# Windowed attention into a three-way maxout layer on one core: x of chunk 1 scaled between masks, V of chunk 2 loaded behind weight 2, half a y moved ahead of products with V

## The chip, the cores and the metric

The kernel runs on one core of one Trainium2 chip. The metric is the time of one execution on the device in microseconds (us). The engines are named as in the profile: PE (matrix products), PEld (its weight loads, which overlap PE), DVE (vector), ACT (scalar, activation), POOL (GpSimd) and SP (which issues most of the transfers).

## The reference

Attention of 4 batches, 8 heads, 768 tokens and head size 64, in which a query sees the first 4 keys (the sink) and the last 128 keys up to itself; its output, 3072 tokens of 512 values, goes through a layer that takes the maximum of three products and then a last product.

```python
scores = scale * np.matmul(q, k.transpose(0, 1, 3, 2))
keep = is_sink | in_window                       # first 4 keys, or 0 <= i - j < 128
a = softmax(np.where(keep, scores, -1000000000.0))
x = np.matmul(a, v).transpose(0, 2, 1, 3).reshape(B * S, H * D)
h = np.maximum(np.maximum(x @ w1, x @ w2), x @ w3)   # 512 -> 768
out = h @ w_out                                       # 768 -> 512
```

## The kernel before

The tokens are worked in 12 chunks of 256, three to a batch. For a chunk, the steps are these, each with a helper that emits its instructions.

- `load` issues the transfers of q, k and V of a chunk on SP, 512 KB each, into raw tiles of which there are two per kind. A `gate` is a tiny write by POOL into the tile; SP's transfer has to wait for it. The gate `after(wi, c)` copies one value of weight `wi` (counted from 0) at column `c`, so it opens only when that piece of the weight has landed.
- `load_w` and `load_wo` load the three weights in thirds, and the output weight in halves, on POOL's queue, which also turns them into bf16.
- `cast_qk` and `cast_v` turn raw tiles to bf16 on POOL, ACT or DVE; `turn` transposes q or k on PE and copies the result out of PSUM; later chunks are transposed by a transfer (`turn_dma`).
- `score` multiplies keys with queries for a pair of heads (p from 0 to 3); `expo` takes two exponentials per pair on ACT; `mask` multiplies by a 0/1 mask on DVE. Pairs 0 and 1 of chunk 1, and the pairs of chunk 0, are masked ahead of their scores by a product with the identity (`premask`), and need no `mask`. `sink_score` and `sink_v` do the same for the four sink keys.
- `av_open` takes four PSUM banks, the o tiles, and writes the sink's share; `av` adds the products of a pair with V, whose last column is one and so gives the row sums. Then DVE takes the reciprocal (L476) and scales x (L479), and the bank is returned.
- `xpose` transposes x in four blocks of 128 columns, one per pair, for each of two halves of the chunk, and copies them to xT (L493).
- `ffn_h(ci, fp, wi)` makes 8 products of 256 columns of chunk `ci`, a third `fp` of the 768 columns and weight `wi` (L517). For weight 0, ACT copies them to h (L523); for the others DVE takes the maximum with h (L527).
- `ffn_y(ci, t)` makes half a chunk of output, 6 products of 512 columns (L540), copied to y by ACT or DVE (L542).

All engines run the written order of the program: the calls stand in one list by hand, each engine takes its own instructions from it in that order, and waits at the first whose operands aren't there. The change edits this list from chunk 1's products with V (L706) to chunk 3's scores (L810). From chunk 4 on a loop repeats one order per chunk.

PSUM has eight banks, shared by everything that PE writes. `bank` takes the one that was returned first, `give` returns it in the order of the program, and the taker waits on the chip until the last reader of the former content is done:

```python
def bank(shape, dtype, name):
    j = free.pop(0)
```

So a call that is moved shifts which bank each later call gets, and on whose reading it depends.

Of the kernel before, what the change touches and what calls it, by code (L numbers as in the profile page):

```python
# [16 lines left out]
def kernel(  # L17
# [13 lines left out]
    nc = tc.nc  # L31
# [12 lines left out]
    DS = d_model // 128  # L44
# [4 lines left out]
    with tc.manual_schedule():  # L49
# [43 lines left out]
        def load(ci, what="kqv", gate=None, part=None, parts=1, eng=None):  # L93
            if ci >= NCH:
                return
            b, c = divmod(ci, CPB)
            t0 = c * 256
            for w in what:
                src = {"k": k, "q": q, "v": v}[w]
                if (ci, w) not in raws:  # L100
                    raws[ci, w] = raw.tile([128, H, 2, D], F32, tag=w + "_raw", name=w + "_raw")
                dst = raws[ci, w]
                if gate is not None:
                    gate(dst[0:1, 0, 0, 0:1])
                n = H // parts
                for g in range(parts) if part is None else (part,):
                    (eng or nc.sync).dma_start(
                        out=dst[:, n * g:n * g + n],
                        in_=src[b, n * g:n * g + n, t0:t0 + 256]
                            .rearrange("h (p i) d -> p h (i d)", i=2))  # L110
# [102 lines left out]
        addm0 = const.tile([128, 3, 128], BF16, name="addm0")  # L213
# [75 lines left out]
        def load_w(wi, c0=0, c1=None):  # L289
            c1 = d_ff if c1 is None else c1  # L290
            w = (moe_w1, moe_w2, moe_w3)[wi]
            nc.gpsimd.dma_start(out=w_sb[wi][:, :, c0:c1],  # L292
                                in_=w.rearrange("(a p) f -> p a f", p=128)[:, :, c0:c1])
# [107 lines left out]
        def mask(ci, p, eng=None):  # L401
            if ci >= NEW:
                return mask4(ci, p)
            lo = 0 if ci % CPB else 1
            e = es[ci, p][0]
            (eng or nc.vector).tensor_mul(e[:, :, lo:], e[:, :, lo:], msk0[0] if lo else msk)  # L406
# [36 lines left out]
        os_ = {}  # L443

        def av_open(ci):
            b, c = divmod(ci, CPB)
            for p in range(NP):
                os_[ci, p] = bank([128, 2, 2, D + 1], F32, "o")
            if c:
                for t in range(2):  # L450
                    for p in range(NP):
                        hp = slice(32 * p, 32 * p + 32)
                        nc.tensor.matmul(  # L453
                            os_[ci, p][:, t], lhsT=es[ci, "sink"][hp, t], rhs=vs[b % 2][hp],
                            start=(t == 0), stop=False, skip_group_check=True,
                            tile_position=(32 * p, 0))

        xs = {}

        def av(ci, p):  # L460
            b, c = divmod(ci, CPB)
            o = os_[ci, p]
            e = es[ci, p][0]
            first = c == 0
            for t in range(2):
                for a in range(2):
                    blocks = [(1, ci, 0)] if t == 0 else [(2, ci, 0), (3, ci, 1)]
                    if t == 0 and c:
                        blocks = [(0, ci - 1, 1)] + blocks
                    for s, cv, n in blocks:  # L470
                        nc.tensor.matmul(  # L471
                            o[:, t, a], lhsT=e[:, a, s], rhs=vb[cv % RING][:, n, 2 * p + a],
                            start=first, stop=True, skip_group_check=True)
                        first = False
            rc = work.tile([128, 2, 2], F32, tag="rc", bufs=4, name="rc")
            nc.vector.reciprocal(rc, o[:, :, :, D])  # L476
            if ci not in xs:
                xs[ci] = work.tile([128, NP, 2, 2, D], BF16, tag="x", bufs=2, name="x_sb")
            nc.vector.tensor_mul(xs[ci][:, p], o[:, :, :, 0:D],  # L479
                                 rc.unsqueeze(3).to_broadcast([128, 2, 2, D]))  # L480
            give(o)

        xTs = {}

        def xpose(ci, t, eng=None):
            eng = eng or nc.scalar
            if t == 0:
                xTs[ci] = work.tile([128, DS, 2, 128], BF16, tag="xT", bufs=3, name="xT")
            pt = bank([128, DS, 128], BF16, "xt")
            for ds in range(DS):  # L490
                nc.tensor.transpose(
                    pt[:, ds], xs[ci][:, ds, t].rearrange("q a d -> q (a d)"), ident)
            (nc.scalar.copy if eng is nc.scalar else eng.tensor_copy)(xTs[ci][:, :, t], pt)  # L493
            give(pt)
# [6 lines left out]

        hs = {}

        def ffn_h(ci, fp, wi, cuts=1, eng=nc.scalar):
            if ci not in hs:
                hs[ci] = work.tile([128, FB, 256], BF16, tag="h", bufs=3, name="h_sb")
            hp = bank([128, 2, 256], F32, "h_ps")
            for f in range(2):
                c0 = (2 * fp + f) * 128
                for ds in range(DS):  # L510
                    x = xTs[ci][:, ds]
                    if ci < NEW:
                        x = x.rearrange("q t (i r) -> q i t r", i=2)
                    else:
                        x = (x.rearrange("q t c -> q (t c)")
                             .rearrange("q (j i r) -> q i j r", i=2, r=32))
                    nc.tensor.matmul(  # L517
                        hp[:, f].rearrange("q (i t r) -> q i t r", i=2, r=x.shape[3]),
                        lhsT=w_sb[wi][:, ds, c0:c0 + 128], rhs=x,
                        start=(ds == 0), stop=(ds == DS - 1))  # L520
            dst = hs[ci][:, 2 * fp:2 * fp + 2]
            if wi == 0:
                (nc.scalar.copy if eng is nc.scalar else eng.tensor_copy)(dst, hp)  # L523
            else:
                for f in range(cuts):
                    x = slice(2 * f // cuts, 2 * (f + 1) // cuts)
                    nc.vector.tensor_max(dst[:, x], dst[:, x], hp[:, x])  # L527
            give(hp)
# [177 lines left out]
        expo(1, 2)  # L706
        load_w(2, 256, 512)
        load_w(2, 512, 768)
        mask(1, 3)
        ffn_h(0, 1, 0)  # L710
        mask(1, 2)
        av_open(1)
        ffn_h(0, 0, 0)
        av(1, 0)
        load(2, 'v', gate=after(0, 300))
        av(1, 3)
        av(1, 1)
        av(1, 2)
        ffn_h(0, 2, 1)
        ffn_h(0, 1, 1)  # L720
        xpose(1, 0, nc.vector)
        xpose(1, 1, nc.scalar)
        ffn_h(0, 0, 1)
        cast_qk(2, 'k', 1, nc.gpsimd)
        ffn_h(1, 2, 0)
        cast_qk(2, 'k', 0, nc.scalar)
        ffn_h(1, 0, 0)
        ffn_h(1, 1, 0)
        load_wo()
        load(3, 'q', gate=after(2, 300))  # L730
        load(3, 'k')
        factors(msk0[0], addm0)
        turn(2, 'k', 0, nc.vector)
        ffn_h(1, 0, 1)
        cast_v(2, 1, 0, nc.gpsimd)
        turn(2, 'k', 1, nc.scalar)
        ffn_h(1, 1, 1)
        cast_qk(2, 'q', 1, nc.scalar)
        cast_qk(2, 'q', 0, nc.vector)
        ffn_h(1, 2, 1)  # L740
        ffn_h(1, 1, 2)
        turn(2, 'q', 1, nc.scalar)
        ffn_h(0, 0, 2)
        turn(2, 'q', 0, nc.scalar)
        ffn_h(0, 1, 2)
        score(2, (0,))
        expo(2, 0)
        score(2, (3,))
        score(2, (1,))
        cast_v(2, 1, 1, nc.gpsimd)  # L750
        sink_score(2)
        expo(2, 1)
        mask(2, 0)
        load(3, 'v', gate=after(1))
        cast_v(2, 0, 0, nc.gpsimd)
        expo(2, 3)
        ffn_h(1, 0, 2)
        cast_v(2, 0, 1, nc.gpsimd)
        ffn_h(0, 2, 2)
        ffn_h(1, 2, 2)  # L760
        score(2, (2,))
        load(4, 'q', gate=after(0, 300))
        cast_qk(3, 'q', 0, nc.gpsimd)
        av_open(2)
        load(4, 'k', gate=after(0))
        mask(2, 1)
        expo(2, 2)
        cast_qk(3, 'k', 0, nc.gpsimd)
        load(4, 'v')
        mask(2, 3)  # L770
        mask(2, 2)
        cast_qk(3, 'q', 1, nc.vector)
        ffn_y(0, 0)
        ffn_y(0, 1)
        av(2, 0)
        turn(3, 'q', 0, nc.scalar)
        cast_qk(3, 'k', 1, nc.scalar)
# [3 lines left out]
        av(2, 3)  # L781
        turn(3, 'q', 1, nc.scalar)
        av(2, 1)
        ffn_y(1, 0)
        turn(3, 'k', 1, nc.scalar)
        turn(3, 'k', 0, nc.scalar)
        xpose(2, 0, nc.scalar)
        xpose(2, 1, nc.vector)
        ffn_y(1, 1)
        cast_qk(4, 'q', 1, nc.vector)  # L790
        cast_v(3, 0, 0, nc.gpsimd)
        cast_v(3, 0, 1, nc.gpsimd)
# [5 lines left out]
        cast_qk(4, 'k', 0, nc.vector)  # L798
        cast_qk(4, 'k', 1, nc.gpsimd)
        mask(3, 1)  # L800
        ffn_h(2, 0, 0)
        cast_v(4, 1, 0, nc.gpsimd)
        cast_v(3, 1, 0, nc.vector)
        score(3, (3,))
        turn_dma(4, 'k')
        turn_dma(4, 'q')
        expo(3, 0)
# [173 lines left out]
```

## Time and profile before

| | us |
|---|---|
| median of 3 runs | 176.03 |
| lowest and highest | 175.41 and 176.61 |
| the profiled execution | 175.3 |
| its span, first to last instruction | 173.6 |
| PE busy | 167.1 |
| DVE busy | 124.7 |
| POOL busy | 110.9 |
| ACT busy | 88.7 |
| bytes moved | 35.22 MB, 203 GB/s over the span |

The profile is of one execution. Line numbers are those of the kernel before. A group row has the line, engine, operation, tiles written and read, shapes and count, then its busy time, the mean of one in ns, and the idle time ahead of it with what ended it. A row of the timeline has start, duration (of so many instructions together), and in square brackets the idle time ahead. The times of one engine can overlap a little, since a row covers an instruction from its first to its last cycle. A row of a transfer ends with the us from issue to landing.

### The profile page before, as it was taken

To read this page: it belongs to the slowest core of one execution; us is meant where nothing else is said; L and a number is where in the kernel's file an instruction comes from. 1 tells how busy PE (TensorE), PEld (TensorE's weight loads), DVE (VectorE), ACT (ScalarE), POOL (GpSimd) and SP (SyncE) were. 2 spreads that over 40 slices of the span, in tenths; PEclk is the share of its full clock that TensorE was granted. 3 is DMA by queue.
4 is the path that set the end of the run, shared out by engine and by line. 5 is a ranking of instruction groups with operands and counts; after the bars stand their busy time and mean duration, and the time that the engine had idled before them with its cause. 6 is when DMAs were issued, how large, how long until landed. Compare 5 with 4: busy or idle time off the path is not lost.

```text
span 173.6 us, 5416 instructions
## 1 busy us (share of the span) xinstructions
PE 167.1 (96%) x2225; PEld 128.6 (74%) x2225; DVE 124.7 (72%) x262; ACT 88.7 (51%) x183; POOL 110.9 (64%) x193
## 2 busy tenths in 40 slices
PE   7979999999999999999999999999999999999992
PEld 2546888857696697797797797797797896896871
DVE  3387854796797985986877976877777776776361
ACT  4778544677954614817726717717636516510210
POOL 7399507545499999999999999999998600000000
PEclk9999999999999999999999999999999999999999
DMA  4999999999999997988999999989999119017303
GB/s 139 301 288 198 218 217 256 221 306 276 280 195 216 190 273 124 245 199 216 253 199 252 195 224 246 265 168 227 264 195 259 32 33 377 21 34 272 121 2 121
DMA packets 71545, 35.22 MB, mean 203 GB/s; under 512 B 27488, under 2 KB 69984, under 8 KB 71520
## 3 DMA queue, kind: packets, MB, share of 16 engines
q1 hardware_dynamic: 65824, 31.60, 79.0%
q0 software_dynamic: 5552, 3.15, 12.7%
q8 instruction: 17, 0.28, 0.7%
q10 hardware_dynamic: 144, 0.13, 0.2%
q14 instruction: 8, 0.07, 0.1%
HBM read 25.17 MB, written 6.29 MB: 181 GB/s over the span
## 4 chain that ended last, share of the span: by engine, by line
PE 85%; DMA 7%; POOL 5%; issue 1%; DVE 0%; POOLq 0%; SPq 0%
PE h_ps L517 52%; PE y_ps L564 11%; PE y_ps L540 7%; PE o L471 6%; DMA w<-in_moe_w_dram 4%; PE st L357 3%; DMA v_raw<-in_v_dram 3%; PE st L331 2%; POOL w L292 2%; POOL vb L123 1%; PE pt L138 1%; PE o L453 1%; PE y_ps L586 1%; PE sk L423 1%; POOL q_bf L118 0%
## 5 line engine op out<-in xcount | busy, mean ns | idle before, releaser
L517 PE MATMUL h_ps<-xT,w 128*128 128x256 bf16 x864 | 101.2, 273 | 0.2 <-DMA w<-in_moe_w_dram 0.2
L517 PEld LDWEIGHTS <-w 128*128 128x128 bf16 x864 | 81.7, 98 | 10.7 <-issue 0.5
L527 DVE TENSOR_TENSOR h_sb<-h_sb,h_ps 128x512 bf16<-128x512 bf16 (+1 forms) x74 | 49.0, 670 | 17.4 <-PE h_ps L517 15.6
L523 ACT CAST h_sb<-h_ps 128x512 bf16<-128x512 f32 x35 | 20.6, 589 | 51.3 <-PE h_ps L517 51.2
L129 POOL CAST vb<-v_raw 32x512 bf16<-32x512 f32 x48 | 36.8, 766 | 2.5 <-DMA v_raw<-in_v_dram 0.3
L90 POOL CAST k_bf<-k_raw 32x512 bf16<-32x512 f32 x48 | 29.6, 616 | 2.2
L398 ACT ACTIVATE e_sb<-st 128x512 bf16<-128x512 f32 (+1 forms) x48 | 23.1, 583 | 1.1 <-PE st L331 1.1
L479 DVE TENSOR_TENSOR x_sb<-o,rc 128x256 bf16<-128x256 f32 x48 | 20.4, 424 | 1.7
L564 PE MATMUL y_ps<-wo,h_sb 64*64 64x512 bf16 (+1 forms) x312 | 21.1, 377 | 0.0
L471 PE MATMUL o<-vb,e_sb 128*128 128x65 bf16 x352 | 16.5, 193 | 0.8 <-DVE vb L123 0.8
L471 PEld LDWEIGHTS <-e_sb 128*128 128x128 bf16 x352 | 14.5, 97 | 3.1 <-ACT e_sb L398 1.0
L123 POOL CAST vb<-v_raw 64x512 bf16<-64x512 f32 x18 | 12.6, 697 | 5.7 <-DMA v_raw<-in_v_dram 5.1
L389 DVE TENSOR_TENSOR e_sb<-e_part,msk 128x1024 bf16<-128x1024 bf16 x16 | 13.1, 831 | 3.3 <-ACT e_part L374 3.1
L406 DVE TENSOR_TENSOR e_sb<-e_sb,msk 128x1024 bf16<-128x1024 bf16 (+1 forms) x18 | 13.6, 776 | 2.3 <-ACT e_sb L398 2.1
L564 PEld LDWEIGHTS <-h_sb 64*64 64x64 bf16 (+1 forms) x312 | 9.9, 106 | 5.0
L374 ACT ACTIVATE e_part<-st 128x384 bf16<-128x384 f32 x32 | 13.1, 495 | 0.5 <-PE st L357 0.5
L540 PE MATMUL y_ps<-wo,h_sb 128*128 128x512 bf16 x54 | 12.8, 380 | 0.0
L476 DVE RECIPROCAL rc<-o 128x4 f32<-128x4 f32 x48 | 8.4, 174 | 4.0 <-PE o L471 3.8
L118 POOL CAST k_bf<-k_raw 128x512 bf16<-128x512 f32 x6 | 3.8, 650 | 9.5 <-PE pt L138 6.8
L118 ACT CAST q_bf<-q_raw 128x512 bf16<-128x512 f32 x13 | 7.6, 620 | 3.0 <-DMA q_raw<-in_q_dram 3.0
L540 PEld LDWEIGHTS <-h_sb 128*128 128x128 bf16 x54 | 4.8, 98 | 5.4 <-DVE h_sb L527 0.8
L427 ACT ACTIVATE e_sink<-sk 128x256 bf16<-128x256 f32 x8 | 3.1, 389 | 10.0 <-PE sk L423 10.0
(90 smaller groups left out, 142.9 us busy)
## 6 DMA issues: line engine op xcount, KB each, us to landing
k_raw<-in_k_dram SPq DMA_DIRECT2D x11, 512.0 KB, 5.6
v_raw<-in_v_dram SPq DMA_DIRECT2D x11, 512.0 KB, 5.6
q_raw<-in_q_dram SPq DMA_DIRECT2D x10, 512.0 KB, 6.9
out_dram<-y_sb SPq DMA_DIRECT2D x9, 512.0 KB, 3.1
w<-in_moe_w_dram POOLq DMA_DIRECT2D x9, 256.0 KB, 6.1
q_raw<-in_q_dram SPq DMA_DIRECT2D x4, 256.0 KB, 7.6
out_dram<-y_sb SPq DMA_DIRECT2D x1, 1024.0 KB, 5.3
wo<-in_moe_w_out_dram POOLq DMA_DIRECT2D x2, 384.0 KB, 8.0
```

Of the source, the lines that this page charges most:

```text
L90: f(bfs[ci, "k"][x:x + 32, :, n], raws[ci, "k"][y:y + 32, :, i].rearrange("q (p a) d -> q p a d", a=2))
L123: eng.tensor_copy(vb[ci % RING][64 * i:64 * i + 64, n, :, 0:D], raws[ci, "v"][64 * n:64 * n + 64, :, i])
L129: eng.tensor_copy(vb[ci % RING][x:x + 32, n, :, 0:D], raws[ci, "v"][y:y + 32, :, i])
L398: nc.scalar.activation(e[:, a, lo:], st[a][:, lo:], AF.Exp, scale=scale)
L406: (eng or nc.vector).tensor_mul(e[:, :, lo:], e[:, :, lo:], msk0[0] if lo else msk)
L471: nc.tensor.matmul(o[:, t, a], lhsT=e[:, a, s], rhs=vb[cv % RING][:, n, 2 * p + a], start=first, stop=True, skip_group_check=True)
L479: nc.vector.tensor_mul(xs[ci][:, p], o[:, :, :, 0:D], rc.unsqueeze(3).to_broadcast([128, 2, 2, D]))
L517: nc.tensor.matmul(hp[:, f].rearrange("q (i t r) -> q i t r", i=2, r=x.shape[3]), lhsT=w_sb[wi][:, ds, c0:c0 + 128], rhs=x, start=(ds == 0 ...
L523: (nc.scalar.copy if eng is nc.scalar else eng.tensor_copy)(dst, hp)
L527: nc.vector.tensor_max(dst[:, x], dst[:, x], hp[:, x])
L540: nc.tensor.matmul(yp, lhsT=hs[ci][:, fb, t * 128:(t + 1) * 128], rhs=wo[:, fb], start=(fb == 0), stop=(fb == FB - 1))
L564: nc.tensor.matmul(yps[ci][t][c:c + cols], lhsT=hs[ci][hp, fb, x:x + cols], rhs=wo[hp, fb], start=(turn == 0 and fb == 0), stop=(turn == 1 ...
```

## The change

In the list of calls:

- The products with V of chunk 1 move up, those of pairs 0 and 1 ahead of the masks of pairs 3 and 2. The scaling of x is split off as `norm`, and stands between the masks and behind other products. The two transposes of xT take their blocks in the order 0, 1, 3, 2.
- The maximum of `ffn_h(0, 2, 1)` is split off as `ffn_max` and put behind the copies of xT.
- `load(2, 'v')` moves from ahead of the products with V to behind `load_wo` and the mask factors, with a gate on the last third of weight 2 in place of weight 0. The load of V of chunk 3, and those of q and k of chunk 4, move up. Two of the four casts of V of chunk 2 go from POOL to DVE, and the other two move down.
- Groups of h products are reordered: `ffn_h(0, 0, 1)` two groups later, `ffn_h(1, 0, 1)` ahead of the transposes of k, `ffn_h(0, 0, 2)` ahead of a transpose of q, and `ffn_h(1, 0, 2)` ahead of the scores of chunk 2.
- `ffn_y(1, 0)` moves ahead of all products with V of chunk 2, and `ffn_y(1, 1)` ahead of its transposes. `score(3, (3,))` moves ahead of `ffn_h(2, 0, 0)`.

```diff
-        def av(ci, p):
+        def av(ci, p, then=True):
...
+            if then:
+                norm(ci, p)
+
+        def norm(ci, p):
+            o = os_[ci, p]
             rc = work.tile([128, 2, 2], F32, tag="rc", bufs=4, name="rc")
             nc.vector.reciprocal(rc, o[:, :, :, D])
...
-        def xpose(ci, t, eng=None):
+        def xpose(ci, t, eng=None, order=range(DS)):
...
-        def ffn_h(ci, fp, wi, cuts=1, eng=nc.scalar):
+        def ffn_h(ci, fp, wi, cuts=1, eng=nc.scalar, then=True):
...
+            maxima[ci, fp, wi] = hp
+            if then:
+                ffn_max(ci, fp, wi, cuts, eng)
+
+        def ffn_max(ci, fp, wi, cuts=1, eng=nc.scalar):
+            hp = maxima.pop((ci, fp, wi))
             dst = hs[ci][:, 2 * fp:2 * fp + 2]
...
         load_w(2, 512, 768)
+        av_open(1)
+        av(1, 0, then=False)
+        av(1, 1, then=False)
         mask(1, 3)
         ffn_h(0, 1, 0)
+        norm(1, 0)
         mask(1, 2)
-        av_open(1)
+        av(1, 3, then=False)
         ffn_h(0, 0, 0)
-        av(1, 0)
-        load(2, 'v', gate=after(0, 300))
-        av(1, 3)
-        av(1, 1)
-        av(1, 2)
-        ffn_h(0, 2, 1)
+        norm(1, 1)
+        av(1, 2, then=False)
+        norm(1, 3)
+        ffn_h(0, 2, 1, then=False)
+        norm(1, 2)
+        xpose(1, 0, nc.vector, (0, 1, 3, 2))
+        xpose(1, 1, nc.scalar, (0, 1, 3, 2))
+        ffn_max(0, 2, 1)
         ffn_h(0, 1, 1)
-        xpose(1, 0, nc.vector)
-        xpose(1, 1, nc.scalar)
-        ffn_h(0, 0, 1)
         cast_qk(2, 'k', 1, nc.gpsimd)
         ffn_h(1, 2, 0)
         cast_qk(2, 'k', 0, nc.scalar)
         ffn_h(1, 0, 0)
+        ffn_h(0, 0, 1)
         ffn_h(1, 1, 0)
+        ffn_h(1, 0, 1)
         load_wo()
+        factors(msk0[0], addm0)
+        load(2, 'v', gate=after(2, 600))
         load(3, 'q', gate=after(2, 300))
         load(3, 'k')
-        factors(msk0[0], addm0)
+        load(3, 'v', gate=after(1))
         turn(2, 'k', 0, nc.vector)
-        ffn_h(1, 0, 1)
-        cast_v(2, 1, 0, nc.gpsimd)
+        ffn_h(1, 1, 1)
         turn(2, 'k', 1, nc.scalar)
-        ffn_h(1, 1, 1)
...
         ffn_h(1, 1, 2)
+        ffn_h(0, 0, 2)
         turn(2, 'q', 1, nc.scalar)
-        ffn_h(0, 0, 2)
+        ffn_h(0, 1, 2)
         turn(2, 'q', 0, nc.scalar)
-        ffn_h(0, 1, 2)
+        ffn_h(1, 0, 2)
         score(2, (0,))
         expo(2, 0)
         score(2, (3,))
         score(2, (1,))
-        cast_v(2, 1, 1, nc.gpsimd)
         sink_score(2)
         expo(2, 1)
         mask(2, 0)
-        load(3, 'v', gate=after(1))
+        expo(2, 3)
+        load(4, 'q', gate=after(0, 300))
+        load(4, 'k', gate=after(0))
+        cast_v(2, 1, 0, nc.gpsimd)
         cast_v(2, 0, 0, nc.gpsimd)
-        expo(2, 3)
-        ffn_h(1, 0, 2)
-        cast_v(2, 0, 1, nc.gpsimd)
         ffn_h(0, 2, 2)
         ffn_h(1, 2, 2)
         score(2, (2,))
-        load(4, 'q', gate=after(0, 300))
         cast_qk(3, 'q', 0, nc.gpsimd)
         av_open(2)
-        load(4, 'k', gate=after(0))
...
         mask(2, 2)
+        cast_v(2, 1, 1, nc.vector)
+        cast_v(2, 0, 1, nc.vector)
         cast_qk(3, 'q', 1, nc.vector)
         ffn_y(0, 0)
         ffn_y(0, 1)
+        ffn_y(1, 0)
         av(2, 0)
...
         av(2, 1)
-        ffn_y(1, 0)
         turn(3, 'k', 1, nc.scalar)
         turn(3, 'k', 0, nc.scalar)
+        ffn_y(1, 1)
         xpose(2, 0, nc.scalar)
         xpose(2, 1, nc.vector)
-        ffn_y(1, 1)
...
         mask(3, 1)
+        score(3, (3,))
         ffn_h(2, 0, 0)
         cast_v(4, 1, 0, nc.gpsimd)
         cast_v(3, 1, 0, nc.vector)
-        score(3, (3,))
```

More of the change, by code (lines that the diff above doesn't have):

```diff
@@ L489, in xpose @@
             pt = bank([128, DS, 128], BF16, "xt")
-            for ds in range(DS):
+            for ds in order:
                 nc.tensor.transpose(
@@ L502 @@
         hs = {}
-        def ffn_h(ci, fp, wi, cuts=1, eng=nc.scalar):
+        maxima = {}
+        def ffn_h(ci, fp, wi, cuts=1, eng=nc.scalar, then=True):
             if ci not in hs:
```

## The prediction

> **What bounds the kernel now.** I read the page's busy shares and costliest groups first, then a table by stage, then the chain that ended last, and only then single engines around the edited lines.
>
> ```profile
> span 173.6 us, 5416 instructions
> PE 167.1 (96%) x2225; PEld 128.6 (74%) x2225; DVE 124.7 (72%) x262; ACT 88.7 (51%) x183; POOL 110.9 (64%) x193
> L517 PEld LDWEIGHTS <-w 128*128 128x128 bf16 x864 | 81.7, 98 | 10.7 <-issue 0.5
> ...
> 16.80:36.90 20.10, 19.93 (x244) 16.63 (x244) 13.62 (x27) 11.61 (x23) 9.44 (x19) 1.00 1.28 235
> 36.90:46.30 9.40, 9.40 (x105) 5.77 (x105) 6.83 (x18) 7.39 (x15) 4.62 (x8) 1.00 1.06 282
> 46.30:170.20 123.90, 123.90 (x1739) 98.69 (x1737) 94.33 (x186) 58.14 (x124) 84.42 (x135) 1.00 0.85 189
> ```
>
> The stage table's columns are the stretch, its length, and the busy time of PE, PEld, DVE, ACT and POOL, then clock, DMA share and GB/s. All edited lines run between 16.8 and 46.3 us. There PE is idle for 0.17 us in all, and after 46.3 it is never idle. Since a busy PE may still be waiting inside, I check it against the chain (start, length, what):
>
> ```profile
> 16.59 6.10 DMA w<-in_moe_w_dram
> ...
> 22.73 3.67 PE h_ps L517 x32
> ...
> 32.60 0.77 PE st L331 x18
> 33.37 0.22 PE sk L423 x4
> 33.59 2.73 PE h_ps L517 x24
> 36.32 0.33 PE st L331 x6
> 36.65 0.23 PE o L453 x8
> 36.87 2.70 PE y_ps L540 x12
> 39.57 0.24 PE o L471 x8
> ...
> 40.98 1.29 PE y_ps L540 x6
> 42.28 0.45 PE pt L138 x8
> ...
> 44.91 0.98 PE h_ps L517 x8
> ...
> 76.24 4.37 PE h_ps L517 x40
> ```
>
> In the undisturbed stage 40 products of h take 4.37 us, 0.109 us each, so 8 take 0.87. By that measure 32 should take 3.50 and took 3.67, 24 should take 2.62 and took 2.73, 8 took 0.98, and 12 products of y took 2.70 where twice 1.29 is 2.58. The hidden stalls in these rows are about 0.1 us each. **PE's order of work sets the end.** The edit removes no matmul, so it can win only such crumbs, and every new wait of PE before 46.3 goes one for one into the time: behind it there is no gap to absorb it.
>
> **The change, part by part.** I walk PE's new order and ask at each step which operand or PSUM bank comes last. Banks go round first in, first out, in the order of the program, so I replayed takes and returns for the new order by hand.
>
> ```profile
> 16.61 2.11 ACT L398 ACTIVATE e_sb<-st 128x512 bf16<-128x512 f32 x4
> ...
> 17.84 0.69 DVE L406 TENSOR_TENSOR e_sb<-e_sb,msk 128x1024 bf16<-128x1024 bf16 x1 [0.22 <-ACT e_sb L398]
> 19.68 0.18 DVE L476 RECIPROCAL rc<-o 128x4 f32<-128x4 f32 x1 [0.24 <-PE o L471]
> ...
> 20.24 0.17 DVE L476 RECIPROCAL rc<-o 128x4 f32<-128x4 f32 x1
> ...
> 17.15 1.05 PE L517 MATMUL h_ps<-xT,w 128*128 128x256 bf16 x8
> ...
> 21.95 0.61 PE L491 MATMUL xt<-ident,x_sb 128*128 128x128 bf16 x8
> ```
>
> *Chunk 1's products with V ahead, x scaled between the masks.* The opening of the o banks now stands right behind the scores, at 17.15, where an h product stood. Its fourth bank is the one that the first of the four exponentials from 16.61 returns, at about 17.2: **+0.1**. The products of pairs 0 and 1 wait for no mask, since those pairs were masked before their scores. DVE then does mask, scale, mask, scale, scale, scale: from 17.84, with 0.65 for a mask and 0.56 for a scaling (19.68 to 20.24), the last one ends near 17.84 + 2 x 0.65 + 4 x 0.56 = 21.4. PE has from 17.25 the rest of the opening (0.23), four products with V (0.24 each) and three groups of 8 h products (0.87 each), so it reaches the transposes near 21.05, takes blocks 0, 1 and 3 first (0.17), and waits for block 2: **+0.2** (bounds 0, if DVE starts earlier, and 0.5).
>
> *What that wait replaces.* Before, the transposes ended at 21.95 + 0.45 = 22.40, and the next h product started at 22.73, when the last piece of weight 1 landed (16.59 + 6.10). In the new order this piece is first read about 2 us later: **-0.33**. The maximum that is put behind the copy of xT costs nothing by itself: DVE would have to wait for the transposes there, and the bank that it returns is taken only several groups of h products later.
>
> *V of chunk 2 behind weight 2.*
>
> ```profile
> v_raw<-in_v_dram SPq DMA_DIRECT2D x1, 512.0 KB, 11.6
> ...
> DMA to landing us min/median/max: 4.1/5.4/11.6
> ...
> w<-in_moe_w_dram POOLq DMA_DIRECT2D x1, 256.0 KB, 11.4
> ...
> q_raw<-in_q_dram SPq DMA_DIRECT2D x1, 512.0 KB, 8.8
> ...
> 20.54 2.05 SPq L107 DMA_DIRECT2D v_raw<-in_v_dram  x1
> ...
> 29.07 1.08 POOL L238 TENSOR_SCALAR msk<-addm 128x384 bf16<-128x384 bf16 x2
> ...
> 32.30 1.27 POOL L123 CAST vb<-v_raw 64x512 bf16<-64x512 f32 x2 [2.16 <-DMA v_raw<-in_v_dram]
> ...
> 40.44 0.62 POOL L118 CAST k_bf<-k_raw 128x512 bf16<-128x512 f32 x1 [1.13 <-DMA k_raw<-in_k_dram]
> ```
>
> V was issued at 20.54 and landed 11.6 us later, at 32.1. The last piece of weight 2, the last of three issues of about 0.75 us from 17.53, lands at about 19.0 + 11.4 = 30.4, so the new gate opens there, behind the mask factors (1.08 us) on POOL, and V is issued near 30.6. Behind that gate on POOL wait the gates of q and V of chunk 3 and of chunk 4, then the casts; on SP all the later loads. Their places in the ring are the same as before (V2, q3, k3, V3, q4, k4). V is first in an emptied ring, beside the output weight. Landing bounds: 30.6 + 4.1, the shortest that the trace has for V, and 30.6 + 11.6, its longest; by bytes, 0.5 MB at half of the 235 GB/s of this stage is 4.5 us, so I take about 36. Two of the four casts of V move from POOL to DVE, at 0.42 us, the price of the same cast there, behind the masks of chunk 2, and end near 39.8; POOL's two end near 37.3. Half a y, 1.29 us, moved ahead puts the first product with V at about 41.2 instead of 39.57, so the late V lies under y: **0**. Without that cover it would cost what V is later than 39.6.
>
> The Trainium skill, "DMA: Bandwidth & Descriptors", section on queues, rings and completion order, says that each DMA engine takes turns between its queue rows, packet by packet. That speaks against the change: by it V, behind q in SP's row, took nothing from weight 2 while q was there, and holding V back brings no weight sooner; the landings (30.4 for the weight, 32.1 for V) agree. Without it weight 2 could land as soon after its issue as weight 1 did, at 25.1, and the gate would open with the factors' end at 30.1, half a us sooner; the sum is the same by both.
>
> *A group of 8 h products of chunk 1 ahead of the scores of chunk 2.*
>
> ```profile
> 31.00 2.47 DVE L527 TENSOR_TENSOR h_sb<-h_sb,h_ps 128x512 bf16<-128x512 bf16 x4
> ...
> 36.96 2.30 DVE L406 TENSOR_TENSOR e_sb<-e_sb,msk 128x1024 bf16<-128x1024 bf16 x3
> ...
> 33.02 1.09 ACT L398 ACTIVATE e_sb<-st 128x512 bf16<-128x512 f32 x2 [0.67 <-PE st L331]
> ...
> 34.26 2.09 ACT L398 ACTIVATE e_sb<-st 128x512 bf16<-128x512 f32 x4
> ...
> 39.60 0.59 ACT L542 COPY y_sb<-y_ps 128x512 f32<-128x512 f32 x1 [0.70 <-PE y_ps L540]
> 40.09 0.59 ACT L142 COPY qT<-pt 128x512 bf16<-128x512 bf16 x1
> 40.56 0.63 ACT L118 CAST k_bf<-k_raw 128x512 bf16<-128x512 f32 x1
> ```
>
> Let S be the start of those scores, 32.60 before. ACT's sixth exponential of that run ends at 34.26 + 2.09 = 36.35, S + 3.75. Before, PE came to the opening of the o banks at 36.65, S + 4.05, behind 24 h products, and lost nothing. Now only 16 stand there: 0.77 + 0.22 + 1.75 + 0.33 puts PE there at S + 3.07, and its fourth bank is the one that this sixth exponential returns. Three small matmuls go first; then PE waits about 0.6 us, less the 0.11 that the 24 products lost before: **+0.5** (bounds +0.2, if a later maximum on DVE delays the 16 products anyway, and +0.7). This is the largest term.
>
> *The half y ahead.* Before, ACT had cast k of chunk 3 by 40.56 + 0.63 = 41.19, well ahead of its transposes at 42.28. Now the copy of that half y stands in front on ACT: y ends at 37.35 + 3 x 1.29 = 41.2; copy, qT copy and cast, started some 0.48 us apart, end at 41.25 + 0.48 + 0.48 + 0.62 = 42.8; PE, 1.41 us of work after 41.2 (39.57 to 40.98 before), is there at 42.6: **+0.25** (0 to 0.5). The y's own 0.12 of stall goes: **-0.1**. The extra score ahead of the first h of chunk 2 takes up the wait for xT that 0.98 against 0.87 shows: 0. POOL behind its cast of k at 40.44 is 0.3 to 1 us later, gives it back in its next wait for a transfer, and has two casts less.
>
> Sum: 0.1 + 0.2 - 0.33 + 0.5 + 0.25 - 0.1 = **+0.6 us**. The profiled execution took 175.3 us with its span of 173.6; it becomes 175.9. The runs' median is 176.03, 0.7 above the profiled one, so the forecast for a median is 176.6.
>
> **The rivals.** *No new wait holds* (the masks start earlier, the banks come in time): the gains alone, 0.33 and 0.1, give 175.6. For it: the terms rest on walks with margins of 0.1 to 0.3 us. Against it: the exponentials' 3.75 us behind S are a fixed row, and PE has only 3.07 us of work to cover them.
>
> *V comes late* and the forecast turns into a clear loss: if V took 11.6 us again it would land at 42.2, POOL's two casts (1.27 us) end at 43.5, and the first product with V, else at 41.2, waits 2.3 us: 176.6 + 2.3 = 178.9. It decides from a landing after 39.9. For it: q and k behind it took 8.8 us and more. Against it: those stood behind V itself in the ring, and now V is first.
>
> *PE has headroom.* The Trainium skill, "Perfetto Trace Analysis", section on the most contended engine, calls matmul busy time a bad measure and the weight loads' share the better one; here that is 74%. As a mechanism of this kernel: if better order let the edited stage's 17 groups of 8 h products run at the weight load's 98 ns instead of 109, that is 136 x 0.011 = 1.5 us and, with the 0.33, 174.2. Against it: 0.109 holds for 40 in a row where nothing is waited for, so order has nothing to do with it.
>
> *The move of V does nothing that it says*: the weights land as before, and V's delay is hidden; the time is then that of the other terms, 176.6.
>
> **How the numbers follow.** Forecast 0.59, no new wait 0.22, V late 0.11, headroom 0.03, the idle move of V 0.05. One per cent is 1.8 us, about what a measurement of this kernel can tell from no change. Only V late lies above it (0.11), only headroom below it (0.03), the others within (0.86). Terms at their lower ends (0.1, 0, -0.33, 0.2, 0, -0.1) give -0.1, at their upper (0.1, 0.5, -0.33, 0.7, 0.5, 0) +1.5, so the forecast's own range is 175.9 to 177.5. With the rival below, the spread of the runs shown (175.41 to 176.61) and part of the way to a late V, the range is 175.3 to 177.9.
>
> **What would show it.** Right: no wait of PE for a weight near 22.7; a short gap of PE before the third block of xT's first transposes; a gap of about half a us at the opening of the o banks near 37, released by ACT; V landed before 39.9; PE's pieces after 46.3 the same, shifted by about 0.6 us. Wrong: PE waiting for a cast of V near 41, DVE's casts of V later than PE's third half of y, or a stage after 46.3 with gaps that it did not have.

## The result and the profile after

| | before | after |
|---|---|---|
| median of 7 runs, us | 176.16 | 176.99 |
| lowest to highest, us | 175.41 to 177.38 | 176.81 to 177.10 |
| the profiled execution, us | 175.3 | 176.99 |
| its span, us | 173.6 | 175.3 |

The ratio of the runs is 1.0052, with a 95% interval of 1.0027 to 1.0077: the change costs 0.5 to 1.4 us, where 0.6 was forecast, and lies inside one per cent. The two profiled executions differ by 1.7 us, twice as much as the medians. That is no contradiction, as the first run below shows: the shown trace of before is one of its shortest executions, the one of after is its median.

The head of the page after, and the table by stage with its bounds moved along:

```profile
span 175.3 us, 5418 instructions
PE 168.9 (96%) x2225; PEld 129.8 (74%) x2225; DVE 126.9 (72%) x264; ACT 89.0 (51%) x183; POOL 108.4 (62%) x191
...
16.80:38.00 21.20, 21.00 (x249) 17.30 (x247) 14.25 (x28) 12.70 (x26) 7.97 (x19) 1.00 1.26 223
38.00:48.00 10.00, 9.62 (x107) 6.17 (x106) 8.18 (x19) 7.01 (x15) 5.43 (x8) 1.00 1.11 289
48.00:171.90 123.90, 123.84 (x1735) 98.31 (x1733) 95.01 (x185) 58.06 (x124) 83.05 (x134) 1.00 0.83 187
```

PE's count of instructions is unchanged, and it is idle for 0.20, 0.38 and 0.06 us in the three stages. POOL lost the two casts that DVE got. The rest of the loss has to be looked for inside PE's busy time, in its timeline:

```profile
16.16 1.03 PE L524 MATMUL h_ps<-xT,w 128*128 128x256 bf16 x8
...
17.45 0.45 PE L453 MATMUL o<-vs,e_sink 32*128 32x130 bf16 x8
17.84 0.66 PE L471 MATMUL o<-vb,e_sb 128*128 128x65 bf16 x16
...
21.44 0.74 PE L496 MATMUL xt<-ident,x_sb 128*128 128x128 bf16 x8
22.01 5.40 PE L524 MATMUL h_ps<-xT,w 128*128 128x256 bf16 x48
...
33.48 1.05 PE L331 MATMUL st<-qT,kT 64*128 64x128 bf16 x18
...
36.92 0.23 PE L453 MATMUL o<-vs,e_sink 32*128 32x130 bf16 x3
37.34 0.27 PE L453 MATMUL o<-vs,e_sink 32*128 32x130 bf16 x5 [0.19 <-ACT e_sb L398]
37.54 4.06 PE L553 MATMUL y_ps<-wo,h_sb 128*128 128x512 bf16 x18
41.44 0.41 PE L471 MATMUL o<-vb,e_sb 128*128 128x65 bf16 x8
...
43.29 0.62 PE L138 MATMUL pt<-ident,k_bf 128*128 128x128 bf16 x8 [0.27 <-ACT k_bf L118]
43.74 1.46 PE L553 MATMUL y_ps<-wo,h_sb 128*128 128x512 bf16 x6
...
47.60 2.79 PE L524 MATMUL h_ps<-xT,w 128*128 128x256 bf16 x24
...
59.98 1.92 PE L524 MATMUL h_ps<-xT,w 128*128 128x256 bf16 x16
```

The 48 products at 22.01 are one unbroken run: no weight is waited for. The opening of the o banks is split into three and five matmuls, and the fourth, the one that the walk named, is released by an exponential on ACT. The transposes of k wait for ACT's cast.

The figure in square brackets is not all that a wait costs, since rows of PE overlap: the 18 products of y end at 41.60 (37.54 + 4.06), and the next row starts at 41.44. From start to start the opening takes 0.62 us here (36.92 to 37.54). Before it took 0.22:

```profile
36.58 0.29 PE L453 MATMUL o<-vs,e_sink 32*128 32x130 bf16 x8
36.80 2.76 PE L540 MATMUL y_ps<-wo,h_sb 128*128 128x512 bf16 x12
```

For all kernels of this document I cut PE's time at five places where each has done the same work: the first h product, the first y, the end of the transposes of k of chunk 3, the start of the 24 h products behind its scores, and its own first h product. The last 72 h products, by the chain, close the table. The columns are lengths in us between these starts, except the first, which is a time.

```text
kernel            first h   to y   to end of k   to 24 h   to h of chunk 3   to last 72 h
before              15.86  20.94          5.76      3.69             12.01         101.50
before, 2nd trace   16.63  22.24          5.76      3.69             12.18         101.51
after               16.16  21.38          6.20      3.86             12.38         101.51
e2                  16.31  21.67          6.20      3.86             12.19         101.51
e3                  16.21  21.17          6.85      3.86             12.21         101.51
e4                  15.79  21.38          6.20      4.02             12.03         101.51
e5                  16.24  21.98          6.65      3.85             12.05         101.51
e6                  15.84  21.33          5.76      3.69             11.92         101.51
e7                  16.00  21.43          7.66      3.69             12.82         101.52
e8                  16.20  20.86          5.96      4.03             13.07         101.50
e9                  15.77  21.54          5.76      3.69             12.23         101.50
e10                 16.32  21.61          5.76      3.69             12.10         101.51
e11                 15.95  20.87          6.65      4.02             12.36         101.51
e12                 15.83  21.39          6.20      3.86             12.63         101.50
```

Between the two shown traces after is longer by 0.44, 0.44, 0.17 and 0.37 us in the four stages, and by 0.30 ahead of the first h product, where the two programs are the same. The stage behind, 101.5 us, is the same in all fourteen traces: what PE loses before it is not given back.

### The profile page after: what moved, and what is told of

Read it like the earlier page. It is cut to its first block, busy times and chain, and to the rows that moved or that the text cites. A ratio compares the mean times of both kernels' runs of the same rounds, so it can differ in the third digit from the quotient of the medians.

```text
span 175.3 us, 5418 instructions
## 1 busy us (share of the span) xinstructions
PE 168.9 (96%) x2225; PEld 129.8 (74%) x2225; DVE 126.9 (72%) x264; ACT 89.0 (51%) x183; POOL 108.4 (62%) x191
## 3 DMA queue, kind: packets, MB, share of 16 engines
q0 software_dynamic: 5552, 3.15, 13.0%
## 4 chain that ended last, share of the span: by engine, by line
PE 87%; DVE 4%; ACT 3%; DMA 3%; issue 1%; ACTq 0%
PE h_ps L524 53%; PE y_ps L577 11%; PE o L471 6%; PE y_ps L553 5%; PE st L357 3%; PE warm L203 3%; DMA xT<-x_sb 3%; ACT e_sb L398 2%; PE pt L138 2%; PE st L331 1%; DVE vb L123 1%; PE o L453 1%; DVE x_sb L484 1%; PE y_ps L599 1%; PE sk L423 1%
## 5 line engine op out<-in xcount | busy, mean ns | idle before, releaser
L90 POOL CAST k_bf<-k_raw 32x512 bf16<-32x512 f32 x48 | 29.1, 607 | 3.4 <-DMA k_raw<-in_k_dram 1.3
L406 DVE TENSOR_TENSOR e_sb<-e_sb,msk 128x1024 bf16<-128x1024 bf16 (+1 forms) x18 | 15.3, 869 | 1.7 <-ACT e_sb L398 1.6
L123 POOL CAST vb<-v_raw 64x512 bf16<-64x512 f32 x16 | 11.4, 713 | 7.4 <-DMA v_raw<-in_v_dram 6.9
L553 PE MATMUL y_ps<-wo,h_sb 128*128 128x512 bf16 x54 | 12.8, 380 | 0.0
```

The costliest lines, as they stand in the source:

```text
L90: f(bfs[ci, "k"][x:x + 32, :, n], raws[ci, "k"][y:y + 32, :, i].rearrange("q (p a) d -> q p a d", a=2))
L123: eng.tensor_copy(vb[ci % RING][64 * i:64 * i + 64, n, :, 0:D], raws[ci, "v"][64 * n:64 * n + 64, :, i])
L553: nc.tensor.matmul(yp, lhsT=hs[ci][:, fb, t * 128:(t + 1) * 128], rhs=wo[:, fb], start=(fb == 0), stop=(fb == FB - 1))
```

## The experiments

**e1, the kernel before, again.**

> The kernel before, unchanged, run against itself. Theory A (the change costs what its new waits of PE cost, about 1 us from 16 to 60 us in the two traces): the median is 176.2 +- 0.3, and a second trace has the same piece of 30.5 us from the first h product to the 24 h products ahead of chunk 3's products with V, give or take 0.2. Rival B (the shown trace of before, 0.9 us under the median of its runs, is a lucky one): the second trace is 0.5 to 1 us longer in that piece, or ahead of it, and the difference of the traces is no measure of the change.

Measured: 175.90 (175.34 to 177.74), ratio 1.0015 (0.9982 to 1.0048). Its profiled execution was one of the longest, 177.55. Its timeline of PE has two waits of which the shown trace had a third of a us of the second alone:

```profile
20.11 1.05 PE L517 MATMUL h_ps<-xT,w 128*128 128x256 bf16 x8 [0.91 <-DMA w<-in_moe_w_dram]
...
24.87 0.39 PE L517 MATMUL h_ps<-xT,w 128*128 128x256 bf16 x2 [0.55 <-DMA w<-in_moe_w_dram]
```

So B holds: the first stage of before is 20.94 or 22.24 us, by when weights 0 and 1 land, and everything behind it is the same to 0.2 us. Of the 2.2 us between the two spans, 1.30 lie in this stage and 0.77 ahead of the first h product. Two traces can't give the size of the change; the medians and the stages have to be read together.

**e2, one group of h products back behind the scores.**

```diff
-        ffn_h(1, 0, 2)
         score(2, (0,))
...
+        ffn_h(1, 0, 2)
         ffn_h(0, 2, 2)
```

> The kernel after, with the one group of h products of chunk 1 (third 0, weight 2) put back behind the scores of chunk 2. Theory A: the opening of the four o banks no longer waits for the exponentials, and the time falls by 0.4 us against after (177.0 to 176.6), with no gap inside the opening (0.23 us instead of 0.69). Rival B (the exponentials set this stage whatever stands behind the scores): PE waits elsewhere before y and the time stays at 177.0.

Measured: 176.80 (176.33 to 177.26), ratio 1.0061 (1.0042 to 1.0081). The opening lost its gap, but the scores, now right behind the last transpose of q, wait for ACT's copy of it:

```profile
33.71 0.84 PE L331 MATMUL st<-qT,kT 64*128 64x128 bf16 x18 [0.67 <-ACT qT L142]
```

The gap moved, by a wait that my edit made, and the first stage is 21.67 us where after has 21.38. The time lies between A's and B's, and this run can't say what the gap costs by itself.

**e3, half a y back behind the products with V.**

```diff
         ffn_y(0, 1)
-        ffn_y(1, 0)
         av(2, 0)
...
         av(2, 1)
+        ffn_y(1, 0)
```

> The kernel after, with half a y of chunk 1 put back behind the products with V. Theory A (that y covers the casts of V on DVE, which end at 41.34 in the trace of after): the first product with V waits from about 40.3 to 41.4, and the stall of 0.26 at the transposes of k goes: 177.0 + 1.0 - 0.3 = 177.7. Rival B (the casts come earlier by themselves when PE does, so that the cover is not needed): 176.7.

Measured: 177.34 (176.77 to 177.63), ratio 1.0091 (1.0071 to 1.0110). The stage from y to the end of k is 6.85 instead of 6.20 us, and its wait stands where A put it:

```profile
41.10 0.39 PE L471 MATMUL o<-vb,e_sb 128*128 128x65 bf16 x7 [0.93 <-DVE vb L123]
```

The half y is a cover that V needs in its late place. The time is nearer A's 177.7 than B's 176.7, and in the stage the loss is 0.65 us where A had 0.7.

**e4, the scores of pair 3 back behind the first h of chunk 2.**

```diff
-        score(3, (3,))
         ffn_h(2, 0, 0)
         cast_v(4, 1, 0, nc.gpsimd)
         cast_v(3, 1, 0, nc.vector)
+        score(3, (3,))
```

> The kernel after, with the scores of pair 3 of chunk 3 put back behind the first h products of chunk 2. Theory A (the moved scores delay ACT's copy of that h, behind it the exponentials and masks of chunk 3, and so the transfer that turns x of chunk 3): the stage behind 47.6 us loses its extra 0.4 us and the first h product of chunk 3 waits 0.1 us for xT as before; at most 0.2 us are lost again at the first h products of chunk 2: 176.7. Rival B (the 0.4 us there come from the transfers' own spread): 177.0.

Measured: 176.80 (176.40 to 177.31), ratio 1.0069 (1.0049 to 1.0089). The stage to chunk 3's h is 12.03 instead of 12.38, the one before it 4.02 instead of 3.86. The signs are those of A, but against after's 1.0052 no gain can be measured.

**e5, the whole block of h groups as before.**

```diff
-        ffn_h(0, 0, 2)
         turn(2, 'q', 1, nc.scalar)
-        ffn_h(0, 1, 2)
+        ffn_h(0, 0, 2)
         turn(2, 'q', 0, nc.scalar)
-        ffn_h(1, 0, 2)
+        ffn_h(0, 1, 2)
         score(2, (0,))
...
+        ffn_h(1, 0, 2)
         ffn_h(0, 2, 2)
```

> The kernel after, with the whole block of h groups around the transposes of q of chunk 2 in the order of before, so that one group stands between the last transpose and the scores, and the group (1, 0, 2) behind them. Theory A (the gap of 0.46 us at the opening of the o banks comes from too few products between scores and opening, and the run with only that one group moved lost its gain to the scores' wait for the copy of qT, 0.66 us): neither wait is left, 177.0 - 0.4 = 176.6. Rival B (the order at the scores does not matter, the time before y is set elsewhere): 177.0.

Measured: 176.73 (176.41 to 177.76), ratio 1.0037 (1.0011 to 1.0064). Inconclusive by time. In its trace the opening takes 0.23 us again and the scores no longer wait for the copy of qT, as A said. But its profiled execution, 177.76, is the longest of twelve; by its chain, q held it up on the way:

```profile
19.63 12.36 DMA q_raw<-in_q_dram
32.04 0.04 issue
32.08 0.44 DVE q_bf L118
```

Its stage from y to the end of k grew from 6.20 to 6.65, as in the run with V and y alone, below: V landed at 38.4 here, 1.3 us later than in after.

**e6, the first part alone, on the kernel before.**

```diff
         load_w(2, 512, 768)
+        load(2, 'v', gate=after(0, 300))
+        av_open(1)
+        av(1, 0, then=False)
...
+        ffn_max(0, 2, 1)
         ffn_h(0, 1, 1)
...
-        ffn_h(0, 0, 1)
...
         ffn_h(1, 0, 0)
+        ffn_h(0, 0, 1)
         ffn_h(1, 1, 0)
```

> The kernel before, with the first part of the change alone: products with V of chunk 1 ahead, x scaled between the masks, the order of the transposes, the maximum behind the copy, and the group (0, 0, 1) two groups later; everything from the load of the output weight on as before, and V of chunk 2 loaded early. Theory A (this part gains the wait for weight 1, 0.33 us in one trace of before and 1.5 us with that for weight 0 in the other, against 0.3 us of new waits): median 175.6 to 175.9, and no run above 177 since the spread of before comes from the weights' landing. Rival B (the gain here is eaten by the new waits at the opening and the transposes of x): 176.0 to 176.3.

Measured: 175.63, and all twelve runs between 175.47 and 175.88; ratio 0.9969 (0.9941 to 0.9997). A holds. It is 0.3% faster than before, by an interval that ends just short of no change, and clearly faster than after; its twelve runs spread over 0.4 us. The timeline of PE shows 40 h products without a wait for a weight, and one small wait, for POOL's cast of k, that after covers with the group (1, 0, 1):

```profile
21.65 4.53 PE L524 MATMUL h_ps<-xT,w 128*128 128x256 bf16 x40
...
27.57 0.40 PE L138 MATMUL pt<-ident,k_bf 128*128 128x128 bf16 x4 [0.29 <-POOL k_bf L118]
```

**e7, V late alone, on the kernel before.**

```diff
-        load(2, 'v', gate=after(0, 300))
...
         load_wo()
+        factors(msk0[0], addm0)
+        load(2, 'v', gate=after(2, 600))
         load(3, 'q', gate=after(2, 300))
```

> The kernel before, with only the load of V of chunk 2 put behind the last third of weight 2 (and the mask factors ahead of it); all casts of V stay on POOL, and y stays behind the products with V. Theory A (V lands near 37 and POOL's four casts end near 40, a little after the first product with V at 39.57; POOL's cast of q of chunk 3 comes late as well): 0.3 to 1.0 us slower than before, 176.2 to 176.9. Rival B (holding V back brings weight 2 and q sooner and pays): 175.5 or less, with the last third of weight 2 landing before 29 us.

Measured: 178.35 (177.84 to 178.59), ratio 1.0120 (1.0077 to 1.0162). Both theories were off, A on the side of too little. On POOL:

```profile
30.81 0.18 POOL L602 CAST v_raw<-w 1x1 f32<-1x1 bf16 x1 [0.54 <-DMA w<-in_moe_w_dram]
...
37.46 1.63 POOL L123 CAST vb<-v_raw 64x512 bf16<-64x512 f32 x2 [6.35 <-DMA v_raw<-in_v_dram]
39.15 0.52 POOL L602 CAST v_raw<-w 1x1 f32<-1x1 bf16 x1
39.62 1.62 POOL L123 CAST vb<-v_raw 64x512 bf16<-64x512 f32 x2
```

and on PE:

```profile
41.30 0.37 PE L471 MATMUL o<-vb,e_sb 128*128 128x65 bf16 x7 [1.07 <-POOL vb L123]
42.17 0.40 PE L138 MATMUL pt<-ident,q_bf 128*128 128x128 bf16 x4 [0.50 <-POOL q_bf L118]
```

The casts took 0.8 us each and had a gate between them, so they ended at 41.2, not at 40; the cast of q behind them was late as well. The stage from y grew by 1.9 us and the one before chunk 3's h by about 0.8: late V, uncovered, is what would have made a clear loss. B falls too: the last third of weight 2 opened its gate at 30.8.

**e8, after with three waits taken out.** The edits of e4 and e5, and ACT's cast of k moved:

```diff
         ffn_y(0, 1)
+        cast_qk(3, 'k', 1, nc.scalar)
         ffn_y(1, 0)
         av(2, 0)
         turn(3, 'q', 0, nc.scalar)
-        cast_qk(3, 'k', 1, nc.scalar)
```

> The kernel after, with three of its waits taken out: the block of h groups as before, the scores of pair 3 of chunk 3 behind the first h products of chunk 2, and ACT's cast of k of chunk 3 ahead of the copy of the half y. Theory A (the waits are separate and add up): 177.0 - 0.4 - 0.2 - 0.25 = 176.1, about the time of before. Rival B (they hide one another, since ACT is behind in all three): 176.6.

Measured: 176.54 (176.11 to 177.59), ratio 1.0038 (1.0016 to 1.0060). The gap at the opening and the wait for k are gone from the first two stages (20.86 and 5.96 us; of the 5.96, 0.2 are again a wait for DVE's cast of V). But the first h products of chunk 2 wait for a copy of xT, as in e4 (4.03), and the stage to chunk 3's h took 13.07, with three waits of PE that after's rows don't name:

```profile
50.08 0.54 PE L471 MATMUL o<-vb,e_sb 128*128 128x65 bf16 x12 [0.25 <-DVE e_sb L406]
...
56.81 1.04 PE L553 MATMUL y_ps<-wo,h_sb 128*128 128x512 bf16 x4 [0.23 <-DVE h_sb L540]
...
60.12 1.92 PE L524 MATMUL h_ps<-xT,w 128*128 128x256 bf16 x16 [0.32 <-DMA xT<-x_sb]
```

The time is B's: a wait that is mended lets PE run into the next one. PE starts the 24 h products at 47.05, 0.55 us earlier than in after, and is through with them at 49.67. The mask ends at 50.04: early enough for after, where the products with V start at 50.23, and too late here. Why x of chunk 3 comes no sooner, this run doesn't show.

**e9, the h block ahead, on the first part.**

```diff
+        ffn_h(0, 0, 2)
         turn(2, 'q', 1, nc.scalar)
-        ffn_h(0, 0, 2)
+        ffn_h(0, 1, 2)
         turn(2, 'q', 0, nc.scalar)
-        ffn_h(0, 1, 2)
+        ffn_h(1, 0, 2)
         score(2, (0,))
...
-        ffn_h(1, 0, 2)
```

> The kernel before with the first part of the change (175.63 in its run, 175.47 to 175.88), and on it the block of h groups around the scores of chunk 2 as after has it, with the group (1, 0, 2) ahead of them. Theory A (too little work stands between the scores and the opening of the o banks, the exponentials need 3.75 us from the scores' start): the opening takes 0.65 to 0.7 us instead of 0.23, and the time rises by 0.4 to 0.5 us to 176.1. Rival B (the gap is filled by waits that were there anyway): 175.7 or less.

Measured: 176.67 (175.93 to 177.73), ratio 1.0046 (1.0024 to 1.0069). The gap at the opening appears with this edit alone:

```profile
36.71 0.23 PE L453 MATMUL o<-vs,e_sink 32*128 32x130 bf16 x3
37.11 0.27 PE L453 MATMUL o<-vs,e_sink 32*128 32x130 bf16 x5 [0.17 <-ACT e_sb L398]
```

Against the next run, on the same chip, the median is 1.0 us up, and the runs spread over 1.8 us. The profiled execution, 176.01, is one of the shortest. Against e6 its first stage is 0.21 us longer and the one to chunk 3's h 0.31, 0.5 in all. A's mechanism holds where it said. The opening takes 0.38 us more than in e6 and the scores ahead of it 0.11 more, 0.5 together; 0.28 of that is hidden in the first stage, because e6 waited that much longer for POOL's cast of k. The 0.31 further on can't be put down to the edit from one trace: the two traces of before differ by 0.17 in the same stage. The median is up by 1.0, and what the longer runs lose beside the gap no trace shows.

**e10, the scores of pair 3 ahead, on the first part.** The edit of e4 the other way.

> The same base, and on it the scores of pair 3 of chunk 3 ahead of the first h products of chunk 2. Theory A (the copy of that h on ACT stands ahead of the exponentials of chunk 3, and the chain mask, scale, transfer of x sets the start of chunk 3's h products, 5.0 us behind its issue): 0.2 to 0.4 us more, 175.9, with a wait for xT at the first h product of chunk 3. Rival B (the chain has room here): 175.6.

Measured: 175.66 (175.51 to 176.47), ratio 0.9982 (0.9957 to 1.0006). B holds: alone the move costs nothing that can be measured.

**e11, V late, its casts on DVE, and both halves of y, on the first part.** This is after with the edits of e4 and e5.

> The same base, and on it V of chunk 2 behind weight 2, two of its casts on DVE, half a y ahead of the products with V, and the other half ahead of the transposes (that is after without the h block and the scores of pair 3 ahead). Theory A (V's delay is covered by y, and what is left is the transposes' wait for ACT's cast of k, 0.25 us, and a later h of chunk 2, 0.2): 175.6 + 0.4 = 176.0. Rival B (V's late place in the ring, which alone cost 2.3 us, is not covered fully): 176.5 or more, with PE waiting for a cast of V or q between y and its products.

Measured: 176.79 (176.45 to 177.11), ratio 1.0052 (1.0036 to 1.0068). The first stage is 0.5 us shorter than in after, and the next 0.45 longer, since PE comes to the products with V before the casts are done:

```profile
36.60 0.29 PE L453 MATMUL o<-vs,e_sink 32*128 32x130 bf16 x8
...
41.20 0.39 PE L471 MATMUL o<-vb,e_sb 128*128 128x65 bf16 x7 [0.29 <-DVE vb L123]
...
43.01 0.62 PE L138 MATMUL pt<-ident,k_bf 128*128 128x128 bf16 x8 [0.25 <-ACT k_bf L118]
```

B is nearer: this part alone costs as much as all that the change lost against e6. The casts of V end at 41.14 here and 41.34 in after; PE comes to the products with V at 40.72 here and 41.44 in after. So the cover holds in after because the gap at the opening has already made PE late.

**e12, after with V early.**

```diff
         load_w(2, 512, 768)
+        load(2, 'v', gate=after(0, 300))
         av_open(1)
...
-        load(2, 'v', gate=after(2, 600))
```

> The kernel after, with only the load of V of chunk 2 back at its early place and gate. Theory A (in after V's delay lies wholly under y and DVE's masks): 177.0, no change, with the opening and the transposes of k waiting as in after. Rival B (V behind weight 2 delays q and k of chunk 3 in the ring and ACT's cast of k with them): 176.5.

Measured: 177.06 (176.33 to 178.01), ratio 1.0075 (1.0048 to 1.0102). A holds: the first three stages are those of after to 0.01 us. In after itself V's delay is covered whole. And it has no gain to show: the last third of weight 2 takes 11.75 us to land with V in flight beside it, and 11.73 in after.

## Why the prediction was right, point by point

*The bound.* Right. The 101.5 us behind the edits are the same in every trace, and each new wait of PE went into the time.

*The opening and the transposes of x.* Forecast +0.1 and +0.2; the opening spans 0.39 us to the first product with V instead of 0.23 and the transposes 0.57 to the next h product instead of 0.45, by the starts above. Right within 0.1.

*The weight's wait, -0.33.* Right in the shown trace, too small for the median: the second trace waited 0.91 and 0.55 us, and the first part alone, whose terms sum to -0.03, took 0.4 us off the median and the whole upper spread. A term that is one execution's arrival time should have had a range, not a value.

*V behind weight 2, 0.* Right in after (e12), for the reason given (e3: without y it costs 0.65 us in its stage). The landing in after, from the list of transfers and DVE's and POOL's timelines:

```profile
v_raw<-in_v_dram SPq DMA_DIRECT2D x1, 512.0 KB, 5.8
w<-in_moe_w_dram POOLq DMA_DIRECT2D x1, 256.0 KB, 11.7
...
31.15 0.18 POOL L615 CAST v_raw<-w 1x1 f32<-1x1 bf16 x1 [0.92 <-DMA w<-in_moe_w_dram]
...
37.26 1.63 POOL L123 CAST vb<-v_raw 64x512 bf16<-64x512 f32 x2 [4.79 <-DMA v_raw<-in_v_dram]
...
37.30 3.15 DVE L406 TENSOR_TENSOR e_sb<-e_sb,msk 128x1024 bf16<-128x1024 bf16 x3
40.48 0.86 DVE L123 CAST vb<-v_raw 64x512 bf16<-64x512 f32 x2
```

V landed 5.8 us after its issue at 31.36, at 37.1, a us later than estimated, and the weight it was held back for took 11.7 us, no less than before. In the six traces with V early it took 11.4 to 12.4, in the eight with V late 11.2 to 12.8. The gate buys nothing, which is the rival of the idle move. But DVE's casts ended at 41.34, not 39.8, 0.1 us ahead of the first product with V: the margin that I had put at 1.4 us was almost none, and in e11, where PE came half a us earlier against the casts, it was gone. Of the 1.5 us, 0.2 are a slip of my sum (masks that end at 39.2 and two casts of 0.42 give 40.0), 0.3 a later start of the masks, and 0.85 their longer time, for which see the last section. The sign that I had named for being wrong, DVE's casts later than PE's third half of y, was missed by 0.1 us, and that is luck.

*The h block, +0.5.* Right, and shown by runs with and without it: the opening takes 0.62 us instead of 0.22, and the first stage is 21.38 with the block and 20.87 without it, in e11. The reason holds too. In the five traces with the block ahead, the first y starts 4.06 to 4.10 us behind the scores, whatever the time of the opening (0.48 to 0.89): the exponentials set it, as the fixed row said. The sixth of them ends 3.82 us behind the scores' first start in the shown traces of both kernels. In the nine without it PE needs 4.27 to 4.45 us there, of which the moved group is 0.87. The first stage as a whole was 21.38 us where the sum (20.94 + 0.1 + 0.2 - 0.33 + 0.5) gave 21.4, which is closer than the terms deserve: the piece from the scores to y lost 0.66 against the shown trace of before, 0.16 more than forecast, and 0.2 came back in pieces that I had not named.

*The half y on ACT, +0.25, and its own stall, -0.1.* The wait for the cast of k is there, and for the reason given, but it is the whole of the 0.44 us by which the stage is longer, where 0.15 was forecast. ACT could copy the half y only at 41.64, when its last product had ended, 0.2 us behind the start of the next row on PE (41.44); I had left that tail out. And the gain of 0.1 could not come: I had read the stall from rows of the chain, which run from end to end. From start to start, 12 products of y took 2.60 us before (36.80 to 39.40) against 2.58, and 18 took 3.90 after: there was hardly a stall. The same holds for the 32 products at 22.73, which took 3.50 and not 3.67.

*Behind that, 0.* Missed: 0.17 at the first h products of chunk 2 and 0.37 up to those of chunk 3. The second is also one of the signs that I had named for being wrong, a stage after 46.3 with gaps that it did not have. In after's chain ACT copies the other half y before it can copy xT, and later PE waits for the transfer of x:

```profile
37.61 4.01 PE y_ps L553 x18
...
45.24 0.59 ACT y_sb L555
45.83 0.50 ACT xT L498
46.32 0.04 issue
46.36 1.03 PE h_ps L524 x8
...
54.97 4.97 DMA xT<-x_sb
59.94 0.05 issue
59.98 1.92 PE h_ps L524 x16
```

The walk had stopped at 46.8. The first I had called taken up by the extra score. The table takes it apart: that stage is 3.69 in all kernels where `ffn_y(1, 1)` stands in its old place, 4.02 or 4.03 where it is moved and the score is not (e4, e8, e11), and 3.85 or 3.86 where both are. So the moved half y costs 0.33, and the score takes up half of it. The second, a transfer of 5.0 us behind DVE's last scaling, was outside what I read. How much of the 0.37 the edit makes stays open: the same stage took 11.92 to 12.23 us in kernels without any edit there (before twice, e6, e9), and the moved scores alone cost nothing in e10.

Together the terms that were too small (0.3 in y's stage, 0.5 behind it) and the one that was too small with the other sign (the weights' landing) nearly cancel in the medians: +0.83 measured, +0.6 forecast. The bound, the gap at the opening and the wait for k are what the forecast had right; that the sum came so near is partly luck, since between the two shown traces these four stages lost 1.42 us.

## What to carry to other kernels

Where one engine's order sets the end, walk the new order on it and ask at each step which operand or returned bank comes last: that found the gap at the opening to 0.1 us, and the place and cause of the wait for the cast of k, whose size it missed by 0.2. Count lengths from start to start: a row that runs from end to end shows stalls that aren't there. Walk on to the end of the last chain that the edit can touch, and give margins for engines that get more work. And before a mend is built, look for the next wait behind it: in e8 and e11 PE only came earlier to a wait that the mended one had hidden. A composite change is worth taking apart; here its first part gains 0.3%, and the rest gives back more than that.

## What the runs showed of the hardware

DVE's three masks of chunk 2 took 3.15 us in after, about 2.5 of it beside POOL's casts (1.63 us for two of V, then 0.85 for one of q). Before they took 2.30, beside one cast of 0.74 us, and POOL's two casts of V, away from the masks, 1.27. In e12, where POOL's cast of q began only at 38.41 and lay beside the third mask alone, they took 1.89:

```profile
37.98 0.74 POOL L118 CAST q_bf<-q_raw 128x512 bf16<-128x512 f32 x1 [2.36 <-DMA q_raw<-in_q_dram]
...
37.12 1.89 DVE L406 TENSOR_TENSOR e_sb<-e_sb,msk 128x1024 bf16<-128x1024 bf16 x3
```

The first row is from before, the second from e12. Over all fourteen traces, each mask of chunk 2 that had no cast of POOL beside it took 0.68 or 0.69 us, and each that took more than 0.9 had at least half a us of such a cast beside it; some with a cast beside them still took 0.68, and why those were spared stays open. The Trainium skill, "GPSIMD Engine Reference", section on specifications, says that POOL shares its SBUF interfaces with DVE, with contention when DVE has two SBUF inputs, as a mask has. The rows agree, and the 0.85 us are more than half of what DVE's casts of V were later than the forecast.
